# Attention score products over 80 and 81 rows or over all 128, with one column of the queries cleared

## The chip, the cores and the metric

The kernel runs on one core of a Trainium2 chip. The metric is the device time of one execution in microseconds (us). The core has TensorE (PE in the profile; its weight loads are PEld), VectorE (DVE), ScalarE (ACT), GpSimd (POOL) and SyncE (SP), which here only issues DMAs.

## What is computed

Clustered attention for 2 batches of 8 heads (768 tokens, 64 values a head), and behind it two feed-forward layers (512 to 2048 to 512) on the 1536 tokens:

```python
q_assign = np.argmax(np.einsum('bhsd,hcd->bhsc', q_n, c_n), axis=-1)   # 16 clusters, normalized rows
k_assign = np.argmax(np.einsum('bhsd,hcd->bhsc', k_n, c_n), axis=-1)
mask = q_assign[:, :, :, None] == k_assign[:, :, None, :]
scores = scale * np.matmul(q, k.transpose(0, 1, 3, 2))
scores = np.where(mask, scores, -1000000000.0)
scores = scores - np.max(scores, axis=-1, keepdims=True)
attn = np.exp(scores)
attn = attn / (np.sum(attn, axis=-1, keepdims=True) + 1e-09)
x = np.matmul(attn, v)          # heads side by side: 1536 x 512
x = softplus(x @ w_in) @ w_out
x = leaky_relu(x @ w_in2) @ w_out2
```

## The kernel before

The 16 heads are worked off one after the other, with the preparation of a head two heads ahead of its use. Each operation gets a priority (`at_pri`), and a scheduler, which models the times of all engines as the program is built, writes the order of each engine's instructions from the priorities and its own clock. Every engine then runs its list in that order. The feed-forward steps of the first batch are strewn between the heads of the second batch (`moe_steps`), so that TensorE has something to do; from about 300 us of the span on, the feed-forward layers stand alone.

For each head, queries and keys live in two padded fp16 buffers, `nq` and `nk`, of 128 partitions x 6 x 128 columns. Columns 0 to 63 hold the values (L293). Columns 64 to 79 hold the token's cluster as a one-hot row (L328, L329), scaled so that a pair of different clusters falls far down. Column 80 (`KS1`) of `nk` is always -1 (L742). Column 80 of `nq` takes the row maximum of the head, negated by that -1 in the product (L356), and columns 96 and 97 of `nq` take a flag for rows without a partner (L357). All other columns are zero from the start (L739). There are five `nq` buffers for the first batch and three for the second, and each is used again and again: `nq_87` by heads 0, 5, 8, 11 and 14, `nq_88` by 1, 6, 9, 12 and 15, `nq_89` by 2, 7, 10 and 13.

A head goes through these steps:

- `split` (L293 to L297): ACT writes the values into `nq` and `nk`; a DMA transpose gives `t1`.
- `assign_mm`, `assign_el` (L306 to L333): the cluster products on PE, the argmax in five DVE instructions that end with the one-hot `oh` (L325), ACT's two writes into `nq` and `nk`, and DMA transposes of both: `tq` (L332) and `tk` (L333).
- `emit_s1` (L344 to L351): the first score product, 12 matmuls of 384 columns, over the first `KS1` = 80 rows of `tq` and `tk`. DVE takes the maximum of each (L351). The two score banks `s1` in PSUM come free by that maximum alone.
- `emit_m` (L356 to L359): the maximum into column 80 of `nq`, the flag into columns 96 and 97, and one more DMA transpose of `nq`, now `tm`.
- `emit_s2` (L377, L378): the second score product, a full 128-row matmul for the low parts and one over `KS2` = 81 rows of `tk` and `tm`; ACT takes the exponential (L384) and POOL the low part of it (L386).
- `emit_pv` (L400 to L418) and `emit_norm`: times the values, and division by the sum.

Weights of the feed-forward layers are decoded from 64-bit to 32-bit numbers by DVE (L140 to L146) and split by ACT (L162) and DVE (L163) in between.

Of the kernel before, what the change touches and what calls it, by code (L numbers as in the profile page):

```python
# [30 lines left out]
NQ_BUFS, NK_BUFS, V_BUFS = (3, 2), (2, 1), 3  # L31
# [20 lines left out]
def by_group(table, h):  # L52
    return table[min(h // 2, 4 + (h >= 12))]
# [3 lines left out]
def attn_moe_kernel(  # L57
# [13 lines left out]
    V, S, G, PE = nc.vector, nc.scalar, nc.gpsimd, nc.tensor  # L71
    B, H, SEQ, D = q.shape
# [25 lines left out]
    def atile(shape, dt, tag, h):  # L98
        late, early = BUFS[tag]
        n = turn[tag] = turn.get(tag, -1) + 1  # L100
        if h < H and early and n % (late + early) >= late:
            return ep.tile(shape, dt, tag=tag, name=tag, bufs=early)
        return at.tile(shape, dt, tag=tag, name=tag, bufs=late)
# [23 lines left out]
    def ring(tag, h=NH):  # L127
        if h < H and tag == "s2":
            n = turn["ps" + tag] = turn.get("ps" + tag, -1) + 1
            if n % (PSUM_BUFS[tag] + 1) == PSUM_BUFS[tag]:  # L130
                return pm.tile([128, 512], F32, tag="m1", name="m")
        return pr.tile([128, 512], F32, tag=tag, name=tag, bufs=PSUM_BUFS[tag])
# [181 lines left out]
    def assign_el(h):  # L314
        nq, nk = nq_of[h], nk_of[h]
        aps = as_t.pop(h)
        a, e = (aps[:, n:n + 2 * C * NCL].rearrange("p (i j) -> p i j", j=NCL) for n in (0, 2 * C * NCL))
        mx = atile([128, 2 * C, 1], F32, "mx", h)
        V.reduce_max(out=mx, in_=a, axis=AX)
        V.tensor_tensor(out=e, in0=a, in1=mx.to_broadcast([128, 2 * C, NCL]), op=ALU.is_equal)  # L320
        V.tensor_tensor(out=e, in0=e, in1=tab, op=ALU.mult)
        m2 = atile([128, 2 * C, 1], F32, "m2", h)
        V.reduce_max(out=m2, in_=e, axis=AX)
        oh = atile([128, C, 2, NCL], F16, "oh", h)
        V.tensor_tensor(  # L325
            out=oh.rearrange("p c t j -> p (c t) j"), in0=e, in1=m2.to_broadcast([128, 2 * C, NCL]), op=ALU.is_equal
        )
        S.activation(out=nq[:, :, D:D + NCL], in_=oh[:, :, 0, :], func=AF.Copy, scale=BIG, bias=-BIG)  # L328
        S.activation(out=nk[:, :, D:D + NCL], in_=oh[:, :, 1, :], func=AF.Copy, scale=BIG)  # L329
        tk = atile([128, C, 128], F16, "tk", h)  # L330
        t = atile([128, C, 128], F16, "tq", h)
        nc.sync.dma_start_transpose(out=t, in_=nq.rearrange("p c d -> p (c d)"))  # L332
        nc.sync.dma_start_transpose(out=tk, in_=nk.rearrange("p c d -> p (c d)"))  # L333
        tp2[h] = t, tk

    KS1 = D + NCL
    KS2 = D + NCL + 1

    def emit_s1(h, c):
        t, tk = tp2[h]  # L340
        for j in range(2):
            bank = ring("s2" if h == 0 and j else "s1", h)
            o = bank[:, 0:3 * 128].rearrange("p (c r) -> p c r", c=3)
            PE.matmul(  # L344
                out=o,
                lhsT=t[0:KS1, c, :],
                rhs=tk[0:KS1, 3 * j:3 * j + 3, :],
                start=True,
                stop=True,
            )  # L350
            V.reduce_max(out=mms[h % 2][:, c, j:j + 1], in_=bank[:, 0:3 * 128], axis=AX)  # L351
# [10 lines left out]
    def emit_s2(h, kt):  # L362
        t1 = tp1[h].rearrange("p (c t) r -> p c t r", t=2)
        t2 = tp2[h][1]
        tqh = tpq[h]
        eng = by_group(PLO, h)[kt]
        p = atile([128, 2, 384], F32, "p", h)
        pl = atile([128, 2, 384], F16, "pl", h) if eng != "P" else None
        pb = p.bitcast(BF16).rearrange("p a (r t) -> p (a r t)", t=2)
        if eng == "D":  # L370
            pb = pb[:, 0:768].rearrange("p (a r) -> p a r", a=2)
        else:
            pb = pb.rearrange("p (a r t) -> p a r t", a=2, t=2)[:, :, :, 1]
        for j in range(2):
            sp = ring("s2", h)[:, 0:384]
            o = sp.rearrange("p (c r) -> p c r", c=3)
            PE.matmul(out=o, lhsT=t1[:, kt, 1, :], rhs=t1[:, 3 * j:3 * j + 3, 0, :], start=True, stop=False)  # L377
            PE.matmul(out=o, lhsT=t2[0:KS2, kt, :], rhs=tqh[0:KS2, 3 * j:3 * j + 3, :], start=False, stop=True)  # L378
            if eng == "D":
                S.activation(out=sp, in_=sp, func=AF.Exp, scale=scale)  # L380
                S.copy(out=pb[:, j, :], in_=sp)
                V.tensor_tensor(out=pl[:, j, :], in0=sp, in1=pb[:, j, :], op=ALU.subtract)
            else:
                S.activation(out=p[:, j, :], in_=sp, func=AF.Exp, scale=scale)  # L384
        if eng == "G":
            G.tensor_tensor(out=pl, in0=p, in1=pb, op=ALU.subtract)  # L386
        p_t[h, kt] = p, pb, pl
# [330 lines left out]
    with at_pri(-9):  # L718
# [6 lines left out]
            out=ss[:, 1:2], in0=ss[:, 0:1], scalar1=ss[:, 2:3], scalar2=ss[:, 1:2], op0=ALU.mult, op1=ALU.add  # L725
# [139 lines left out]
    def chain(h):  # L865
        if h < NH:
            with at_pri(h - LEAD_SPLIT):
                split(h)
            with at_pri(h - LEAD_ASSIGN):
                assign_mm(h)  # L870
                assign_el(h)
            with at_pri(h - LEAD_MAX):
                for c in range(C):
                    emit_s1(h, c)
            with at_pri(h - LEAD_M):
                emit_m(h)
            if h + 2 < NH:
                with at_pri(h - LEAD_LOAD):
                    load(h + 2)
# [12 lines left out]
    for h in range(NH):  # L892
        chain(h + AHEAD)
        wtie["h"] = h + 1
        with at_pri(h):
            if h + 1 < NH:
                split_v(h + 1)
            if h + 2 < NH:
                with behind_tm(h + 1):
                    load_v(h + 2)  # L900
            emit_sv(h)
        for j in range(C):
            with at_pri(h + j / 6):
                emit_s2(h, j)
                if j:
                    emit_pv(h, j - 1)
            if h < H - 1 and (j + h * C) % W_PER == 0:
                w_step()
            if h > H or (h == H and j > 0):
                moe_steps(FF_RATE)  # L910
            if h == H and j == 0:
                open_late()
        with at_pri(h + 1):
            emit_pv(h, C - 1)
            emit_empty(h)
        with at_pri(h + 1 - LEAD_NORM):
            emit_norm(h)
# [49 lines left out]
```

## Time and profile before

| | us |
|---|---|
| runs of the kernel (3) | 751.99, 756.89, 762.72 |
| median | 756.89 |
| the profiled execution's own time | 753.12 |
| its span, first to last instruction | 751.3 |
| mean granted TensorE clock over the span | 0.968 of full |

The span is what the rows below are read from; 1.8 us of the profiled execution's time lie around it. Rows are times in us from the start of the span. A granted clock of 1.00 is TensorE's upper level of 2.4 GHz, 0.50 the lower of 1.2 GHz. A matmul's duration runs from its start until its result is in PSUM, so matmuls that follow each other overlap, and busy time of PE says that something was in flight, not that it ran at its best.

### The profile page before, as it was taken

The page shows a single profiled execution, that of the slowest core. Times are in us where ns is not written, and L with a number is a line of the kernel's source. Part 1 is how long each engine was busy: PE and PEld are TensorE (multiplying, and loading weights), DVE is VectorE, ACT ScalarE, POOL GpSimd, SP SyncE. Part 2 cuts the span into 40 slices and gives each one's busy share as a digit, 9 for nine tenths or more (in the row PEclk, how much of TensorE's full clock was granted, in tenths as well). Part 3 has the DMA queues.
Part 4 walks back from the last instruction along what each step waited for, and adds up shares of the span by engine and source line. Part 5 has one row for each costly group of instructions (what it writes and reads, how often), then busy time and mean ns, then how long its engine had stood idle before and what let it go on. Part 6 is the DMA issues. An engine that isn't in the chain of part 4 may idle for free.

```text
span 751.3 us, 18834 instructions
## 1 busy us (share of the span) xinstructions
PE 689.3 (92%) x7488; PEld 509.8 (68%) x7488; DVE 515.0 (69%) x1154; ACT 402.6 (54%) x1071; POOL 400.0 (53%) x491
## 2 busy tenths in 40 slices
PE   1799888988888898999999999999999999999997
PEld 1368566655555565666666566656999999999996
DVE  4777667677788887029878866976476666666555
ACT  5465555566777766136335434534555555565553
POOL 4386567658788777211324342333646555656563
PEclk9988899998999999999999999999999999999999
DMA  8966656955785866012322355696100000000000
GB/s 199 195 133 148 127 124 108 189 123 126 185 186 141 156 155 161 14 22 66 120 96 64 106 181 169 181 357 218 74 2 30 2 30 2 30 2 30 2 30 29
DMA packets 118088, 81.01 MB, mean 108 GB/s; under 512 B 91888, under 2 KB 106224, under 8 KB 118000
## 3 DMA queue, kind: packets, MB, share of 16 engines
q1 hardware_dynamic: 117856, 79.55, 41.5%
q8 instruction: 58, 0.95, 0.5%
q14 instruction: 30, 0.25, 0.1%
q10 hardware_dynamic: 144, 0.26, 0.1%
HBM read 50.36 MB, written 10.49 MB: 81 GB/s over the span
## 4 chain that ended last, share of the span: by engine, by line
PE 55%; DVE 16%; DMA 12%; ACT 6%; POOL 5%; issue 4%; SPq 2%; DVEq 0%; POOLq 0%; ACTq 0%
PE i L538 13%; PE acc L538 13%; PE m L686 11%; PE m L673 6%; DMA t<-n 3%; DMA tm<-nq 2%; DMA v<-in_v_dram 2%; PE s L344 2%; PE s L378 2%; DMA st<-in_moe_w_in_dram 2%; DVE e L513 2%; PE s L377 2%; DVE w_in2l L240 2%; ACT p L384 2%; DVE g_l L487 1%
## 5 line engine op out<-in xcount | busy, mean ns | idle before, releaser
L386 POOL TENSOR_TENSOR pl<-p 128x768 f16<-128x768 f32 x88 | 128.3, 1467 | 56.2 <-ACT p L384 40.8
L351 DVE TENSOR_REDUCE mm<-s 128x1 f32<-128x384 f32 x190 | 101.2, 552 | 41.3 <-PE s L344 39.0
L538 PEld LDWEIGHTS <-w_in2h 128*128 128x128 f16 x1344 | 98.2, 98 | 5.3 <-issue 0.7
L546 DVE TENSOR_TENSOR gl<-r,gh 128x384 f16<-128x384 f32 (+1 forms) x96 | 63.8, 665 | 49.7 <-ACT gh L584 49.1
L384 ACT ACTIVATE p<-s 128x384 f32<-128x384 f32 x160 | 73.4, 493 | 29.1 <-PE s L378 25.4
L673 PE MATMUL m<-xth,w_inh 128*128 128x384 f16 x256 | 85.2, 333 | 3.4 <-ACT rl L497 1.8
L686 PE MATMUL m<-g_h,w_outh 128*128 128x384 f16 x256 | 84.3, 329 | 3.1 <-ACT w_outh L162 2.7
L686 PE MATMUL m<-g_l,w_outh 128*128 128x384 f16 x256 | 84.1, 328 | 2.1 <-DVE g_l L487 2.1
L673 PE MATMUL m<-xtl,w_inh 128*128 128x384 f16 x256 | 85.1, 333 | 0.0
L686 PE MATMUL m<-g_h,w_outl 128*128 128x384 f16 x256 | 84.0, 329 | 0.0
L546 POOL TENSOR_TENSOR r<-r,r 128x128 f32<-128x128 f32 x95 | 48.3, 526 | 55.7 <-ACT r L576 55.4
L673 PEld LDWEIGHTS <-w_inh 128*128 128x128 f16 x512 | 50.5, 100 | 36.9 <-issue 6.1
L344 PE MATMUL s<-tk,tq 80*128 80x384 f16 x190 | 65.0, 364 | 11.3 <-DMA tk<-nk 5.6
L686 PEld LDWEIGHTS <-w_outh 128*128 128x128 f16 x512 | 49.9, 99 | 37.2 <-ACT w_outh L162 3.6
L584 ACT CAST gh<-r 128x384 f16<-128x384 f32 (+1 forms) x96 | 54.2, 565 | 36.0 <-POOL r L546 32.6
L538 PEld LDWEIGHTS <-gh 128*128 128x128 f16 x672 | 60.5, 98 | 6.4 <-issue 1.1
L378 PE MATMUL s<-tm,tk 81*128 81x384 f16 x160 | 55.0, 354 | 8.7 <-DMA tm<-nq 8.7
L377 PE MATMUL s<-t 128*128 128x384 f16 x160 | 56.5, 353 | 3.7 <-ACT p L384 3.5
L200 POOL TENSOR_TENSOR wd<-wd 128x256 f32<-128x256 f32 x32 | 29.3, 924 | 54.5 <-DVE sg L194 39.8
L538 PE MATMUL i<-sh,w_in2h 128*128 128x128 f16 x384 | 53.5, 219 | 0.4 <-ACT r L576 0.4
L538 PE MATMUL i<-sl,w_in2h 128*128 128x128 f16 x384 | 53.5, 219 | 0.0
L538 PE MATMUL i<-sh,w_in2l 128*128 128x128 f16 x384 | 53.4, 219 | 0.0
(146 smaller groups left out, 1926.2 us busy)
## 6 DMA issues: line engine op xcount, KB each, us to landing
st<-in_moe_w_in_dram SPq DMA_DIRECT2D x32, 512.0 KB, 4.5
st<-in_moe_w_out_dram SPq DMA_DIRECT2D x32, 512.0 KB, 3.8
kept<-sg SPq DMA_DIRECT2D x16, 256.0 KB, 2.8
qk<-in_q_dram SPq DMA_DIRECT2D x16, 192.0 KB, 3.0
qk<-in_k_dram SPq DMA_DIRECT2D x16, 192.0 KB, 3.0
v<-in_v_dram SPq DMA_DIRECT2D x16, 192.0 KB, 4.2
kept<-sg SPq DMA_DIRECT2D x24, 128.0 KB, 2.8
out_dram<-ob SPq DMA_DIRECT2D x11, 256.0 KB, 2.3
```

What stands on the lines that cost most here:

```text
L200: G.tensor_tensor(out=out, in0=in0, in1=in1, op=ALU.subtract)
L344: PE.matmul(out=o, lhsT=t[0:KS1, c, :], rhs=tk[0:KS1, 3 * j:3 * j + 3, :], start=True, stop=True,)
L351: V.reduce_max(out=mms[h % 2][:, c, j:j + 1], in_=bank[:, 0:3 * 128], axis=AX)
L377: PE.matmul(out=o, lhsT=t1[:, kt, 1, :], rhs=t1[:, 3 * j:3 * j + 3, 0, :], start=True, stop=False)
L378: PE.matmul(out=o, lhsT=t2[0:KS2, kt, :], rhs=tqh[0:KS2, 3 * j:3 * j + 3, :], start=False, stop=True)
L384: S.activation(out=p[:, j, :], in_=sp, func=AF.Exp, scale=scale)
L386: G.tensor_tensor(out=pl, in0=p, in1=pb, op=ALU.subtract)
L538: one = PE.matmul(out=bank, lhsT=w_, rhs=x_, start=(first and i == 0), stop=(i == len(ops) - 1), skip_group_check=True)
L546: eng.tensor_tensor(out=out, in0=in0, in1=in1, op=op)
L584: S.copy(out=gh[:, lo:hi], in_=r[:, lo:hi])
L673: PE.matmul(out=hp, lhsT=w_, rhs=x_, start=(i == 0), stop=(i == len(ops) - 1))
L686: PE.matmul(out=yp, lhsT=w_[:, kk, ms], rhs=g_[:, kk, :], start=(n == 0), stop=(n == 3 * KFF - 1))
```

## The change

Both score products use all 128 rows of their operands. The rows that come in are zero in `tk` (columns 81 to 127 of `nk`), so they add nothing; but the first product now takes in row 80 as well, where `tk` holds -1, and `tq` would hold the maximum of the head that had the buffer before. So column 80 of `nq` is cleared by DVE ahead of the transpose, for the heads whose buffer was used before: heads 5, 6, 7 and 8 to 15, 11 in all.

```diff
@@ assign_el
+        if h >= (sum(NQ_BUFS) if h < H else H):
+            V.memset(nq[:, :, KS1:KS2], 0.0)
         S.activation(out=nq[:, :, D:D + NCL], in_=oh[:, :, 0, :], func=AF.Copy, scale=BIG, bias=-BIG)
@@ emit_s1
             PE.matmul(
                 out=o,
-                lhsT=t[0:KS1, c, :],
-                rhs=tk[0:KS1, 3 * j:3 * j + 3, :],
+                lhsT=t[:, c, :],
+                rhs=tk[:, 3 * j:3 * j + 3, :],
                 start=True,
@@ emit_s2
-            PE.matmul(out=o, lhsT=t2[0:KS2, kt, :], rhs=tqh[0:KS2, 3 * j:3 * j + 3, :], start=False, stop=True)
+            PE.matmul(out=o, lhsT=t2[:, kt, :], rhs=tqh[:, 3 * j:3 * j + 3, :], start=False, stop=True)
```

Lines from L328 on stand two lines further down in the changed kernel (the memset is its L329). The new instruction moves the scheduler's clock, so the lists of all engines differ in places from the middle of head 0 on.

On DVE, around the maximum of head 5 (`nq_87`), the kernel before has this order; `mm` are the maxima of the first score product, `svr` belongs to the sum of the values, `x` to the division of the head before:

```order
L351 TENSOR_REDUCE mm_101<-s_1587 128x1
L356 TENSOR_REDUCE nq_87<-mm_102 128x6
L351 TENSOR_REDUCE mm_101<-s_1590 128x1
L351 TENSOR_REDUCE mm_101<-s_1593 128x1
L430 SCALAR_TENSOR_TENSOR svr<-h_1941,sel,as 32x65
L351 TENSOR_REDUCE mm_101<-s_1596 128x1
L351 TENSOR_REDUCE mm_101<-s_1599 128x1
L351 TENSOR_REDUCE mm_101<-s_1602 128x1
L351 TENSOR_REDUCE mm_101<-s_1605 128x1
L447 TENSOR_SCALAR x<-x 128x6
```

At the same place the changed kernel has this:

```order
L358 TENSOR_REDUCE nq_87<-mm_102 128x6
L353 TENSOR_REDUCE mm_101<-s_1589 128x1
L353 TENSOR_REDUCE mm_101<-s_1592 128x1
L353 TENSOR_REDUCE mm_101<-s_1595 128x1
L353 TENSOR_REDUCE mm_101<-s_1598 128x1
L353 TENSOR_REDUCE mm_101<-s_1601 128x1
L432 SCALAR_TENSOR_TENSOR svr<-h_1944,sel,as 32x65
L329 MEMSET nq_87 128x6
L353 TENSOR_REDUCE mm_101<-s_1604 128x1
```

The memset for head 8 stands six instructions behind the maximum of head 5 in the same buffer. It may not overwrite the buffer before the transpose `tm` of head 5 has read it, and everything behind it on DVE waits as well.

On DVE, around the maximum of head 1 (`nq_88`), the kernel before has:

```order
L356 TENSOR_REDUCE nq_88<-mm_102 128x6
L351 TENSOR_REDUCE mm_101<-s_408 128x1
L351 TENSOR_REDUCE mm_101<-s_411 128x1
L319 TENSOR_REDUCE mx<-as 128x12
L351 TENSOR_REDUCE mm_101<-s_414 128x1
```

and the changed kernel:

```order
L358 TENSOR_REDUCE nq_88<-mm_102 128x6
L353 TENSOR_REDUCE mm_101<-s_405 128x1
L353 TENSOR_REDUCE mm_101<-s_408 128x1
L329 MEMSET nq_88 128x6
L353 TENSOR_REDUCE mm_101<-s_411 128x1
L319 TENSOR_REDUCE mx<-as 128x12
```

Here the memset for head 6 stands only two maxima behind the maximum of head 1. The other nine stand two to ten instructions behind the maximum of the head that had the buffer.

## Rows read from the trace of the kernel before

**Rows 1.** The page's slices of the span: granted clock in tenths
```profile
PEclk9988899998999999999999999999999999999999
```

**Rows 2.** Windows: stretch, its length, busy time of each engine, PEclk, DMA share, GB/s
```profile
30.00:300.00 270.00, 235.18 (x2940) 161.93 (x2940) 205.01 (x442) 173.15 (x428) 195.65 (x167) 0.92 0.67 149
300.00:751.00 451.00, 442.60 (x4427) 341.88 (x4423) 291.18 (x642) 215.58 (x609) 192.70 (x297) 1.00 0.24 78
```

**Rows 3.** The page's costliest groups: the three kinds of score matmul
```profile
L344 PE MATMUL s<-tk,tq 80*128 80x384 f16 x190 | 65.0, 364 | 11.3 <-DMA tk<-nk 5.6
...
L378 PE MATMUL s<-tm,tk 81*128 81x384 f16 x160 | 55.0, 354 | 8.7 <-DMA tm<-nq 8.7
L377 PE MATMUL s<-t 128*128 128x384 f16 x160 | 56.5, 353 | 3.7 <-ACT p L384 3.5
```

**Rows 4.** Windows of all engines, columns as in rows 2: three stretches and their successors
```profile
105.40:108.80 3.40, 2.26 (x23) 1.49 (x23) 1.30 (x4) 2.25 (x6) 1.64 (x2) 1.00 1.08 233
108.80:112.20 3.40, 3.40 (x22) 1.92 (x21) 1.51 (x4) 2.31 (x6) 2.39 (x3) 0.50 0.64 185
187.30:190.70 3.40, 2.31 (x33) 1.41 (x29) 0.08 (x1) 3.09 (x8) 3.40 (x4) 1.00 0.88 271
190.70:194.10 3.40, 1.29 (x16) 0.71 (x13) 2.27 (x4) 1.16 (x3) 1.91 (x2) 1.00 1.24 234
218.00:221.40 3.40, 1.79 (x26) 1.23 (x25) 3.21 (x7) 1.40 (x5) 1.80 (x3) 1.00 0.99 262
221.40:224.80 3.40, 3.40 (x41) 2.24 (x40) 2.52 (x6) 3.35 (x11) 3.33 (x4) 1.00 0.45 102
```

**Rows 5.** Windows of L344 on PE alone: busy time, PEclk, DMA share, GB/s
```profile
105.40:108.80 3.40, 0.87 (x4) 1.00 1.08 233
...
218.00:221.40 3.40, 0.65 (x2) 1.00 0.99 262
```

**Rows 6.** Windows of L378 on PE alone, columns as in rows 5
```profile
105.40:108.80 3.40, 1.30 (x5) 1.00 1.08 233
187.30:190.70 3.40, 1.31 (x4) 1.00 0.88 271
218.00:221.40 3.40, 0.74 (x3) 1.00 0.99 262
```

**Rows 7.** The chain, shares of 50.7-61.0, 78.1-84.9, 108.8-112.2, 173.6-180.5, in this order
```profile
by line: PE x L400 25.4%; PE s L344 17.0%; PE s L377 9.3%; PE x L413 9.1%; PE x L414 8.9%; PE x L418 6.4%; PE s L378 6.2%; DVE wcp L143 5.9%; DVE mm L351 4.6%; PE m L377 3.1%; PE m L378 3.1%; PE as L425 3.1%; PE as L424 2.7%; issue 0.4%
by line: PE s L377 25.9%; PE s L378 23.5%; PE s L344 18.4%; PE m L378 11.8%; PE m L377 11.1%; PE x L436 6.5%; PE x L418 4.9%; issue 0.3%
by line: PE s L344 23.9%; PE s L377 18.8%; PE s L378 18.8%; PE m L377 16.8%; PE x L413 9.8%; PE x L414 9.6%; PE m L378 9.4%
by line: DMA t<-n 102.3%; PE m L673 49.9%; PE as L306 11.7%; PE s L377 9.5%; PE s L378 9.3%; PE s L344 9.3%; issue 0.7%
```

**Rows 8.** Line L742: the only small memset of one column
```profile
L742 DVE MEMSET nk<- x3: 63/63/63, 8.3 to 8.4; 128x6 f16 x3
```

**Rows 9.** Timeline of DVE, 100.5 to 108: start, duration, instruction, idle time before it
```profile
100.71 0.18 DVE L356 TENSOR_REDUCE nq<-mm 128x6 f16<-128x18 f32 x1
...
103.50 1.53 DVE L351 TENSOR_REDUCE mm<-s 128x1 f32<-128x384 f32 x3 [0.32 <-PE s L344]
107.39 0.56 DVE L351 TENSOR_REDUCE mm<-s 128x1 f32<-128x384 f32 x1 [2.36 <-PE s L344]
```

**Rows 10.** The chain, 100 to 108: start, duration, what
```profile
102.24 4.26 DMA tm<-nq
```

**Rows 11.** Timeline of DVE, 41.5 to 46
```profile
43.67 0.36 DVE L319 TENSOR_REDUCE mx<-as 128x12 f32<-128x192 f32 x1 [0.22 <-PE as L306]
```

**Rows 12.** Timeline of ACT, 44 to 46
```profile
44.74 0.51 ACT L293 CAST nq<-qk 128x384 f16<-128x384 f32 x1 [0.63 <-DMA tm<-nq]
```

**Rows 13.** Waits of the whole span: us in total, times, longest
```profile
ACT nq L293 <- DMA tm<-nq: 14.1, 9, 3.0
```

## Prediction

> **What bounds the kernel now.** I read the page's clock line first [rows 1], then two windows that split the span [rows 2], then the chain of waits within single stretches. The clock line has its eights in the first third only and nines behind it. The windows say the same in numbers: from 300 us on PE is busy for 442.6 of 451 us at a clock of 1.00, and nothing in this change touches that part. From 30 to 300 us, where the heads run, PE is busy for 235.2 of 270 us at a mean clock of 0.92, and DVE for 205.0, ACT for 173.2, POOL for 195.7. No engine is full there: the chain goes from transposes (one is 4.26 us long [rows 10]) to PE, to DVE's maxima, to ACT's exponentials, and back. So a gain has to come from 30 to 300 us, and the mean clock bounds it: 0.92 at levels of 1.00 and 0.50 means that 0.08 / 0.50 x 270 = 43 us are run at half clock. If PE set the end through all of these, full clock would give back half, 21.6 us. That is the most the clock can give.
>
> **The change part by part.**
>
> *The matmuls themselves.* There are 192 matmuls in L344 and 192 in L378. Their duration doesn't speak for a price of the rows: 364 ns with 80 rows, 354 with 81, and 353 for L377 with all 128 and the same 384 columns [rows 3]. So I put the additional rows at 0 ns. Both sides: 353 - 364 = -11 ns times 384 is -4 us of busy time, 353 - 354 = -1 ns times 384 is -0.4 us; the differences are those of the clock in which the groups happened to run, so no term.
>
> *What the rows may do to the clock.* The granted clock falls behind stretches in which PE has little to do. Three stretches can be compared [rows 4]. From 105.4 to 108.8 PE was busy for 2.26 us, and the clock was 0.50 in the next stretch. From 187.3 to 190.7 it was busy for 2.31 us, and the clock stayed. From 218.0 to 221.4 it was busy for only 1.79 us, and the clock stayed too. So busy time doesn't sort them. What differs is the kind of work: in the first, 4 + 5 = 9 of 23 matmuls were score matmuls over 80 or 81 rows, with 0.87 + 1.30 us of busy time [rows 5, 6]; in the second 4 of 33 (L378's alone), in the third 2 + 3 = 5 of 26. The clock fell where most of the work was done by part of the rows. If what counts is work in rows, the change makes each of these matmuls count for 128, and stretches like the first keep their clock. The Trainium skill speaks against it (TensorE: Matmul & The Clock Gate, section "What's actually happening"): the clock follows how busy PE has been of late, with no word of rows. By that rule alone the change does nothing to the clock, and the term that follows is 0; the three stretches here don't agree with busy time alone, but they are only three.
>
> The price comes from the chain. Four half-clock stretches lie behind waits in which score matmuls of part of the rows were a good part of PE's work: 50.7 to 61.0, 78.1 to 84.9, 108.8 to 112.2 and 173.6 to 180.5. PE's shares of the chain there add up to 94%, 102%, 107% and 90% [rows 7] (pieces at the edges count whole, so a sum can pass 100). Half of that time would go at full clock: 0.94 x 10.3 / 2 = 4.9, 1.02 x 6.8 / 2 = 3.5, 1.07 x 3.4 / 2 = 1.8 and 0.90 x 6.9 / 2 = 3.1, in sum 13.3 us. The rest of the 21.6 us lies in stretches that follow waits with few score matmuls, which should stay, or in which PE isn't on the chain. Of the 13.3 us I take half, 6.6: once PE is quick again, what is late next is DVE's maxima, which are 552 ns apiece against 160 ns for the 384 columns of a matmul at 2.4 GHz, and the two score banks come free by them alone. Ends: 0 and -21.6 us.
>
> *The memset.* Eleven instructions of one column; the like of it took 63 ns [rows 8], so 0.7 us on DVE. Its wait is dearer. Each stands few instructions behind the maximum of the head that had the buffer, and may start only once that head's transpose `tm` has landed. Behind it stand the maxima of the head that is then prepared, behind those PE's next L344 (two banks), and behind that PE's other work, since PE takes its list in order. For head 8: the maximum of head 5 was at 100.71, the rows up to the memset were through at 103.50 + 1.53 = 105.03 [rows 9], and the transpose landed at 102.24 + 4.26 = 106.50 [rows 10]. The memset would wait 1.5 us, but DVE did nothing until 107.39 anyway: PE was itself behind that transpose. There the wait is covered. For head 6 it isn't: DVE went on to L319 at 43.67 [rows 11], and the transpose landed at about 44.74, when ACT's write into the same buffer was released [rows 12]: 1.1 us of DVE lost. ACT's write has the same wait at all places, and there it costs 14.1 us at 9 of them [rows 13]. So the memsets' waits cost DVE between 0 (all covered as at head 8) and some 14 us (none covered). Head 6 is the kind I expect at about a third of the places, 11 / 3 x 1.1 = 4 us of DVE, of which less than half should reach the end, because DVE has 270 - 205 = 65 us of idle time in these stages [rows 2]: 1.5 us, its own 0.7 us included.
>
> *The moved order.* The lists of all engines differ locally; I see no side in it, cost it at 0 and allow 5 us either way.
>
> *The sum.* -6.6 + 1.5 = -5.1 us against the profiled execution's own 753.1 us: 748.0. The median of the runs lies 3.8 us above that execution, so 756.9 - 5.1 = 751.8, in round numbers 752 us.
>
> **The rivals.**
>
> *The rows don't count for the clock.* For it: only three stretches speak for rows, and the third, with the least busy time, kept its clock with 5 score matmuls. Against it: the first has more busy time than the third and fell. Then only the memset is left: 756.9 + 1.5 = 758.4, with the moved order 754 to 764. This is also the case in which the rule of the skill's page holds.
>
> *The memsets' waits decide: slower.* The place is the memset in DVE's list, the price the 14.1 us that ACT loses at the same landings. It decides if DVE comes to the memset before the landing at most of the 11 places and PE isn't itself behind that transpose, so that maxima that would have been made in the wait are late, the two banks stay full, and PE starves at just the place where its clock falls. With no clock gained: 756.9 + 14.1 + 0.7 = 771.7, and each additional half-clock stretch like that at 108.8 adds 1.8 us: up to about 775. For it: head 6, and ACT's longest wait of 3.0 us. Against it: head 8, and DVE's idle time.
>
> *All half clock goes.* If the clock holds through the heads and PE sets the end in these stretches, -21.6 + 1.5 = -20.1 us: 736.8; with a part of it hidden by DVE, about 740. Against it: waits for transposes and weights remain, and stretches without score matmuls such as 190.7 to 194.1 (busy for 1.29 us) gain nothing by rows.
>
> **How the numbers follow.** The forecast has a chance of 0.52 and a range of its own of 745 to 758; the rows that don't count 0.24; the waits 0.11; all half clock gone 0.13. The range of 738 to 769 takes in the first two cases whole and reaches into the other two. A difference of 2% is 15.1 us, about what a measurement of this kernel can tell from no change: faster than 741.8 is most of the last case and a little of the forecast, 0.14; slower than 772.0 is the upper half of the waits' case and what a bad order could add, 0.09; within 2% is what remains, 0.77.
>
> **What would show it.** Right: the clock over 30 to 300 us rises from 0.92 to 0.95 or more, the half clock at the like of 50.7 to 61.0 and 108.8 to 112.2 is gone, L346 and L380 (the new lines of the score matmuls) keep their duration at full clock, and the memsets of L329 last 0.06 us with a few us of DVE idle ahead of them by DMA `tm`. The feed-forward part from 300 us on keeps its length. Wrong: a clock that stays at 0.92 (rows don't count), DVE idle at the memsets in sum near 14 us with PE waiting for `mm` behind it (the waits decide), a clock near 1.00 (all of it goes), or a clock that rises while the heads end no sooner, which would say that PE's speed in those stretches was covered by DVE and the transposes, and that half was too much to take.

## The result, and the profile after

The changed kernel takes 758.46 us (median of 22 runs, 753.57 to 761.75) against 754.44 us for the kernel before on the same chips (749.18 to 762.72). The ratio is 1.0054, with a 95% interval of 1.0033 to 1.0074: 4 us slower, where 5 us faster was forecast. The time lies inside the range, well within 2%, but on the other side of 1. Here and below, times are medians of all executions, and ratios leave out those more than 1.5% above the fastest of their kernel (the profiles of runs 2 and 11 are of such executions, and aren't read).

The profiled execution has a span of 755.9 us. Its clock line, in 40 slices as in [rows 1]:

```profile
PEclk9899999899999999999999999999999999999999
```

Of the four eights in the first third, two are left. In windows, columns as in [rows 2], the heads and the feed-forward part:

```profile
30.00:300.00 270.00, 226.19 (x2931) 156.10 (x2931) 198.96 (x445) 172.38 (x426) 195.82 (x167) 0.95 0.69 145
300.00:756.00 456.00, 443.89 (x4433) 342.58 (x4430) 296.95 (x650) 216.35 (x611) 192.78 (x297) 0.99 0.24 79
```

The clock over the heads rose from 0.92 to 0.95, as the prediction asked. PE's busy time there fell from 235.2 to 226.2 us. But PE also got fewer matmuls done by 300 us, 2931 against 2940, and what is left to do behind 300 us takes 456 us and not 451. PE's time was gained on each matmul and lost between them.

The groups of the page that answer to [rows 3]:

```profile
L346 PE MATMUL s<-tk,tq 128*128 128x384 f16 x190 | 61.6, 345 | 14.0 <-DMA tk<-nk 7.5
...
L380 PE MATMUL s<-tm,tk 128*128 128x384 f16 x160 | 53.0, 339 | 10.8 <-DMA tm<-nq 10.8
L379 PE MATMUL s<-t 128*128 128x384 f16 x160 | 53.6, 337 | 7.5 <-ACT p L386 6.7
```

All three kinds are shorter, L379 too, which the change doesn't touch: that is the clock. The rows themselves have no price. But the idle time of PE ahead of each has grown: from 11.3, 8.7 and 3.7 us (L344, L378, L377) to 14.0, 10.8 and 7.5 (L346, L380, L379).

The memsets, by their line and what DVE waited for ahead of them:

```profile
L329 DVE MEMSET nq<- x11: 63/63/63, 33.0 to 236.9; 128x6 f16 x11
its engine sat idle before it (us, times) until:
  DMA tm<-nq: 4.8, 4
```

63 ns each, and 4.8 us of waits at 4 of 11 places: the size that the prediction drew from head 6 (4 us at a third of the places).

### The profile page after: what moved, and what is told of

Same layout as the page of the kernel before. It is cut to its first block, busy times and chain, and to the rows that moved or that the text cites. A ratio compares the mean times of both kernels' runs of the same rounds, so it can differ in the third digit from the quotient of the medians.

```text
span 755.9 us, 18867 instructions
## 1 busy us (share of the span) xinstructions
PE 680.3 (90%) x7488; PEld 504.2 (67%) x7488; DVE 514.8 (68%) x1165; ACT 402.7 (53%) x1071; POOL 400.3 (53%) x491
## 4 chain that ended last, share of the span: by engine, by line
PE 51%; DMA 17%; DVE 15%; ACT 6%; issue 4%; POOL 4%; SPq 2%; DVEq 0%; POOLq 0%; ACTq 0%
PE acc L540 13%; PE i L540 13%; PE m L675 9%; PE m L688 7%; DMA v<-in_v_dram 3%; DMA t<-n 3%; DMA tm<-nq 3%; DMA st<-in_moe_w_in_dram 3%; DMA st<-in_moe_w_out_dram 2%; DVE mm L353 2%; DMA tk<-nk 2%; PE s L346 2%; DVE w_in2l L240 1%; DVE e L515 1%; PE s L380 1%
## 5 line engine op out<-in xcount | busy, mean ns | idle before, releaser
L346 PE MATMUL s<-tk,tq 128*128 128x384 f16 x190 | 61.6, 345 | 14.0 <-DMA tk<-nk 7.5
L380 PE MATMUL s<-tm,tk 128*128 128x384 f16 x160 | 53.0, 339 | 10.8 <-DMA tm<-nq 10.8
L379 PE MATMUL s<-t 128*128 128x384 f16 x160 | 53.6, 337 | 7.5 <-ACT p L386 6.7
L415 PE MATMUL x<-v,p 128*128 128x65 f16 x528 | 49.8, 198 | 5.4 <-DVE y L452 4.9
```

Source lines behind the costliest of these rows:

```text
L346: PE.matmul(out=o, lhsT=t[:, c, :], rhs=tk[:, 3 * j:3 * j + 3, :], start=True, stop=True,)
L380: PE.matmul(out=o, lhsT=t2[:, kt, :], rhs=tqh[:, 3 * j:3 * j + 3, :], start=False, stop=True)
L415: PE.matmul(out=o, lhsT=pb[:, cs], rhs=v2[:, kt, D:2 * D + 1], start=(kt == 0 and c == 0), stop=False)
```

## The experiments

The experiments separate three things that the change does at once: the rows on the chip, the memset, and the order of the lists. For that some kernels change the rows of the finished matmuls after the scheduler has written its lists, with this helper at the end of the program (`have` picks the matmuls and weight loads, `want` gives their rows):

```python
def rows(have, want):
    for bb in nc.main_func.blocks:
        done = []
        for i in bb.instructions:
            if i.opcode in ("Ldweights", "Matmult") and have(i):
                ins = [type(x)(ap=[(x.ap[0][0], want(i))] + list(x.ap[1:]), offset=x.offset, ...) for x in i.ins]
                i = i.__replace__(ins=ins)
            done.append(i)
        bb.instructions = done
```

Ratios are to the kernel before, run on the same chip in turn.

### 1. The order of before, all 128 rows

```diff
+    rows(lambda i: i.ins[0].ap[0][1] in (80, 81), lambda i: 128)
     r = _run(nc, [arrays], core_ids=[0])
```

> Order of before on every engine, instruction for instruction; only the rows of the two score matmuls are 128 in place of 80 and 81. There is no memset, so in the first product row 80 takes in the maximum of the head that had the buffer before (that part of the computation differs). Theory A (the rows keep the clock up and this is worth time; the loss of the changed kernel is from its moved order): 3 to 7 us faster than before, ratio 0.991 to 0.996, mean clock 0.98 or more. Theory B (the memsets' waits on DVE cost): the same as A here. Theory C (the clock goes up, but what PE gains is covered by transposes and DVE): ratio 0.998 to 1.002 with a clock of 0.98. Theory D (rows don't count for the clock; the rise to 0.978 came from the moved order): clock stays at 0.965 to 0.970, ratio 1.000.

Measured: 749.33 us, ratio 0.9923 (0.9894 to 0.9953). The rows alone, in the same order, are worth 0.77%, 5.8 us. Theory A or B; C (the gain is covered) and D (rows don't count) fall. The clock of before and of this run over the same stretch, first before, then this run (from 37.1 us on, since before's trace holds no clock events earlier):

```profile
37.10:300.00 262.90, 230.24 (x2906) 159.07 (x2905) 201.53 (x433) 169.00 (x417) 192.36 (x164) 0.92 0.67 147
```
```profile
37.10:300.00 262.90, 224.77 (x2935) 155.71 (x2934) 200.93 (x434) 169.76 (x418) 194.22 (x165) 0.96 0.67 149
```

0.08 / 0.50 x 262.9 = 42 us at half clock become 0.04 / 0.50 x 262.9 = 21 us. PE is 5.5 us less busy and has done 29 matmuls more. These are single executions; over the executions of both kernels the median of the mean granted clock rises from 0.970 to 0.981, which is some 16 us of half clock rather than 21.

Single stretches of this run, to be held against those of the prediction:

```profile
50.00:58.00 8.00, 7.49 (x132) 6.07 (x132) 7.87 (x19) 5.50 (x15) 8.00 (x7) 1.00 0.99 190
104.80:108.20 3.40, 3.40 (x16) 1.71 (x15) 2.32 (x7) 2.40 (x6) 1.56 (x3) 0.50 0.95 241
170.00:176.50 6.50, 5.47 (x62) 3.36 (x59) 6.29 (x16) 6.02 (x15) 5.84 (x6) 1.00 0.56 164
```

What ran at half clock from 50.7 to 61.0 and from 173.6 to 180.5 now runs at full clock. The stretch behind the wait that the prediction used as its main example (105.4 to 108.8, now about 3 us earlier) still ran at half: the reason was right in sum, and its own showpiece doesn't bear it out. The two places aren't quite alike, though: half clock now sets in a little earlier in the work, and PE was busy for only 1.40 of the 3.4 us ahead of it, where it had been 2.26.

### 2. The order of the changed kernel, 80 and 81 rows

```diff
+    rows(lambda i: i.debug.lineno in (346, 380), lambda i: {346: 80, 380: 81}[i.debug.lineno])
     r = _run(nc, [arrays], core_ids=[0])
```

> Order and memset of the changed kernel, instruction for instruction; the score matmuls take 80 and 81 rows as before. A: slower than before by 1.0 to 1.5% (the moved order without the rows' gain), clock 0.96. B: likewise 1.0 to 1.5%. C: about 1.005, as with all rows, at a clock of 0.96. D: 1.005 and a clock of 0.978 as in the changed kernel.

Measured: 765.84 us, ratio 1.0097 (1.0054 to 1.0141). Without the rows' gain the changed kernel would be a full percent slower. The granted clock, as the median over the executions that the ratios take, closes the square: 0.970 in both orders with 80 and 81 rows, 0.981 (order of before) and 0.982 (changed order) with 128. So between these two orders the clock follows the rows and not the order (run 6 has a third order, where it rose less), and the loss is in what remains: the memset or the order.

### 3. The memset tied behind its own one-hot

```diff
-        V.tensor_tensor(
+        last = V.tensor_tensor(
             out=oh.rearrange("p c t j -> p (c t) j"), ...
         if h >= (sum(NQ_BUFS) if h < H else H):
-            V.memset(nq[:, :, KS1:KS2], 0.0)
+            with tc.issue_after(last.ins):
+                V.memset(nq[:, :, KS1:KS2], 0.0)
```

> The changed kernel with the memset tied behind the one-hot of its own head, so that it comes one to two heads later in DVE's list, long after the transpose it must wait for. B: DVE's waits for the transpose at the memset (4.8 us at 4 places in the changed kernel) go to 0, and the time falls to a ratio of 0.996 to 1.001. A: the waits go too, but the order moves again, and the time may land anywhere between 0.995 and 1.010; it says nothing alone. C: 1.003 to 1.007, as the changed kernel.

Measured: 758.58 us, ratio 1.0052 (1.0024 to 1.0080), the changed kernel's own. The waits are gone, as the line of the memset shows:

```profile
L330 DVE MEMSET nq<- x11: 63/63/63, 69.7 to 267.8; 128x6 f16 x11
its engine sat idle before it (us, times) until:
who waited for it (us, times):
  ACT nq L331: 0.9, 1
```

No DVE time ahead of it, and no time won. That speaks against B, though the order has moved a little as well; the next run has no such gap.

### 4. The memset at the same place, without the wait

```diff
+    for bb in nc.main_func.blocks:
+        ...
+            if i.opcode == "Memset" and i.debug.lineno == 329:
+                i = i.__replace__(outs=[o], sync_info=type(s)(on_wait=[], on_update=s.on_update))
```

`o` is six elements a partition in the tile `sq`, which nobody reads any more.

> The changed kernel's order, instruction for instruction, with all 128 rows; the 11 memsets stand at the same places of DVE's list but write into a tile nobody reads any more and wait for nothing. So the column isn't cleared, and the first product takes in the old maximum (that part of the computation differs). B: the loss goes, ratio 0.996 to 1.001, since 4.8 us of DVE waits are gone. A: stays at 1.003 to 1.006, since the order is what costs. C: 1.003 to 1.006 too; e1 tells C from A.

Measured: 759.75 us, ratio 1.0058 (1.0029 to 1.0087). Every list is the changed kernel's, 4.8 us of DVE waits are gone, and the time is the same. B falls: within the interval the memsets' waits cost nothing, so they are covered, as at head 8 in the prediction.

### 5. Column 80 cleared by ACT, order of before

```diff
-        oh = atile([128, C, 2, NCL], F16, "oh", h)
+        oh = ohs[h % 2]      # two fixed tiles of NCL + 1 columns, the last set to 1.0 at the start
-            out=oh.rearrange("p c t j -> p (c t) j"), ...
+            out=oh.rearrange("p c t j -> p (c t) j")[:, :, 0:NCL], ...
-        S.activation(out=nq[:, :, D:D + NCL], in_=oh[:, :, 0, :], func=AF.Copy, scale=BIG, bias=-BIG)
+        S.activation(out=nq[:, :, D:D + NCL + 1], in_=oh[:, :, 0, :], func=AF.Copy, scale=BIG, bias=-BIG)
+    rows(lambda i: i.ins[0].ap[0][1] in (80, 81), lambda i: 128)
```

> All 128 rows without the memset and, but for 6 rows of difference near the end of PE's list and the places of a few instructions at the start, in the order of before: the one-hot gets a 17th column that is always 1, ACT's write of the cluster takes it along (32768 x 1 - 32768 = 0) and so clears column 80; the scheduler still sees 80 and 81 rows, and the rows are set to 128 behind it. Theory A (rows gain about 6 us, the moved order costs about 7): ratio 0.989 to 0.996, clock 0.98, faster than both kernels. Rival (the gain of the first run came from the old maximum in row 80 or from the missing clear): 0.998 or more.

Measured: 752.07 us, ratio 0.9953 (0.9922 to 0.9984): faster than before and than the changed kernel, with nothing of the computation left out. It stands a little above the first run (0.9923), but the intervals overlap; this version's clock was 0.976 in the median, between the two levels of the other runs.

### 6. The order that the memset alone makes

The changed source with 80 and 81 rows for the scheduler, and 128 set behind it:

```diff
-                lhsT=t[:, c, :],
+                lhsT=t[0:KS1, c, :],
...
+    rows(lambda i: i.ins[0].ap[0][1] in (80, 81), lambda i: 128)
```

> All 128 rows and the memset, but in the order that the scheduler makes when it sees 80 and 81 rows and the memset; this differs from before's and from the changed kernel's. A1 (what costs in the changed kernel's order is what the row counts did to it): like the first run with the order of before, 0.990 to 0.998. A2 (any move of the order costs, the tuned one being the best of many): 1.000 to 1.006.

Measured: 755.98 us, ratio 1.0001 (0.9972 to 1.0031). Neither clean case: 0.8% above the order of before with the same rows, and 0.5% below the changed kernel. A third order gives back what the rows gain, but not more. Its clock was 0.972 in the median, against 0.970 for the kernel before and 0.976 to 0.979 for the other kernels with 128 rows on the same chip (runs 5, 7 and 8): in this order the rows raised the clock by little. So orders differ by about as much as the rows are worth, and the order also has a say in how much clock the rows give.

### 7. All 128 rows, scheduled as such, no memset

```diff
-        if h >= (sum(NQ_BUFS) if h < H else H):
-            V.memset(nq[:, :, KS1:KS2], 0.0)
```

> All 128 rows, scheduled as such, without the memset: every engine's list is that of the changed kernel, less the 11 memsets on DVE (the first product takes in the old maximum, that part of the computation differs). A: the loss is all in the order that the row counts make, ratio 1.002 to 1.007, as the changed kernel. B (the memset costs, by its wait or otherwise): 1.000 or below.

Measured: 760.85 us, ratio 1.0073 (1.0041 to 1.0105). The lists of PE, ACT, POOL and SP are those of the changed kernel to the instruction, DVE's too but for the 11 memsets. So it isn't the memset that made the changed kernel's order. The row counts alone made the scheduler write other lists, though a matmul over them lasts as long on the chip; what in its model of the engines reacts to the rows stays open.

### 8. Only the second product over 128 rows

```diff
-            PE.matmul(out=o, lhsT=t2[0:KS2, kt, :], rhs=tqh[0:KS2, 3 * j:3 * j + 3, :], start=False, stop=True)
+            PE.matmul(out=o, lhsT=t2[:, kt, :], rhs=tqh[:, 3 * j:3 * j + 3, :], start=False, stop=True)
```

> Only the second product over all 128 rows, the first over 80 as before; no memset is needed. The scheduler's lists differ from before's from head 8 on, hardly ahead of it. A with the loss put between heads 4 and 7 (where the changed kernel loses 8 of its 10 us against the same rows in the order of before): about half of the rows' gain and little loss, 0.993 to 0.999. If the order's loss isn't tied to that place: 1.000 or more.

Measured: 752.82 us, ratio 0.9968 (0.9938 to 0.9997). One line of source, no memset, no helper, and faster than before by 0.3%. All rows that are added here hold zeros in `tk`; the clock was 0.979, against 0.970 for the kernel before on the same chip.

### 9 and 10. Which half of the heads has the loss

`emit_s1` and `emit_s2` take 128 rows where the condition holds and `KS1` or `KS2` where it doesn't; all are set to 128 behind the scheduler.

```diff
+        k1 = 128 if h < H else KS1        # run 10: h >= H
-                lhsT=t[0:KS1, c, :],
+                lhsT=t[0:k1, c, :],
```

> All 128 rows on the chip in all heads, no memset (the first product takes in the old maximum, that part of the computation differs). The scheduler sees 128 rows for heads 0 to 7 and 80 or 81 for heads 8 to 15: the lists are the changed kernel's up to the preparation of head 8, and go their own way behind it. If the order's loss is made ahead of head 8 (theory A with the place at heads 4 to 7): 1.002 to 1.008. If it is made behind: 0.990 to 0.997.

> The reverse: the scheduler sees 80 or 81 rows for heads 0 to 7 and 128 for heads 8 to 15; all are run with 128, no memset (the same part of the computation differs). The lists are before's up to the preparation of head 8. Loss ahead of head 8: 0.989 to 0.996, like the order of before with 128 rows (0.992). Loss behind it: 1.002 or more.

Measured: 1.0033 (1.0002 to 1.0064; 760.96 us) with the changed kernel's lists up to the preparation of head 8, and 0.9952 (0.9917 to 0.9988; 753.12 us) with before's lists up to there. Most of the order's loss is made in the first batch: 1.0033 / 0.9923 = 1.1% in run 9 and 0.9952 / 0.9923 = 0.3% in run 10, the latter inside the intervals. The split is a rough one, since behind head 8 run 9 has lists of its own and not the changed kernel's.

The five lists of run 10 are also those of run 8, instruction for instruction; the two differ in the rows of the first product alone. Their ratios, 0.9952 and 0.9968, and clocks, 0.978 and 0.979, can't be told apart: in this order the second product's rows give what both give.

The place can be seen in the normalization of a head (its product with 1 / sum on DVE). Head 3 and head 7 in the first run, in the order of before with 128 rows:

```profile
92.49 0.56 DVE L450 TENSOR_TENSOR y<-x,dd 128x384 f32<-128x384 f32 x1
...
151.75 0.55 DVE L450 TENSOR_TENSOR y<-x,dd 128x384 f32<-128x384 f32 x1
```

and in the changed kernel:

```profile
94.35 0.56 DVE L452 TENSOR_TENSOR y<-x,dd 128x384 f32<-128x384 f32 x1
...
161.72 0.55 DVE L452 TENSOR_TENSOR y<-x,dd 128x384 f32<-128x384 f32 x1
```

1.9 us behind at head 3, 10.0 us behind at head 7, the last of the first batch. Runs 9 and 10 fall on the two sides: head 7 at 160.8 and at 150.3. The first matmul of the feed-forward work, which fills PE's gaps from then on, comes 10.1 us later too, at 151.6 against 141.5, and the spans of the two kernels differ by 755.9 - 746.3 = 9.6 us in the end. That the loss stays because nothing filled PE's gaps ahead of it is an argument; no run tests it.

The windows between these two points show what PE did, first in the order of before, then in the changed kernel:

```profile
92.50:151.80 59.30, 49.73 (x699) 36.07 (x696) 42.28 (x101) 33.10 (x85) 40.65 (x34) 0.94 0.69 137
```
```profile
94.30:161.70 67.40, 53.33 (x715) 38.86 (x714) 44.66 (x106) 37.26 (x93) 44.05 (x38) 0.92 0.69 129
```

Of the 8.1 us, PE was idle for 4.5 (14.07 against 9.57) and busy for 3.6, at a clock that was lower there, 0.92 against 0.94. The chain between these two points, first in the order of before (92.5 to 151.8), then in the changed kernel (94.3 to 161.7):

```profile
by line: DMA tm<-nq 18.1%; DMA t<-n 15.4%; ACT p L384 8.0%; issue 7.1%; PE s L378 5.8%; PE s L344 5.3%; PE x L400 4.5%; PE s L377 4.5%; POOL pl L386 4.2%; PE as L306 3.7%; PE x L418 2.7%; PE m L377 2.6%; PE x L413 2.3%; PE x L414 2.2%; PE m
```
```profile
by line: DMA v<-in_v_dram 22.5%; DMA tm<-nq 16.9%; DMA tk<-nk 6.8%; ACT p L386 6.3%; PE s L346 6.1%; PE x L402 5.7%; PE s L380 5.6%; issue 5.2%; PE s L379 4.5%; DVE mm L353 3.4%; PE x L415 2.5%; PE x L416 2.2%; PE x L420 1.8%; SPq L361 1.8%
```

The loads of `v` head the second list and are nowhere near the top of the first. On ACT, whose list holds the cast of `v` (L285) at fixed places, that looks so in the changed kernel:

```profile
112.17 0.52 ACT L285 CAST v<-v 128x384 f16<-128x384 f32 x1 [3.08 <-DMA v<-in_v_dram]
...
133.37 0.52 ACT L285 CAST v<-v 128x384 f16<-128x384 f32 x1 [1.57 <-DMA v<-in_v_dram]
```

and in the order of before at the like of the first of them:

```profile
109.90 0.51 ACT L285 CAST v<-v 128x384 f16<-128x384 f32 x1
```

There the cast comes when `v` has long landed; in the changed kernel ACT stands before it for 3.08 and 1.57 us, with exponentials behind it in its list. All waits of this kind between the two points, in the first run and in the changed kernel:

```profile
ACT v L285 <- DMA v<-in_v_dram: 2.0, 2, 1.1
```
```profile
ACT v L285 <- DMA v<-in_v_dram: 6.8, 3, 3.1
```

### 11 and 12. Shorter loads of v in both orders

```diff
+            if i.opcode.startswith("DMA") and i.debug.lineno == 280:      # from the fourth head on
+                a = [(6 * a[0][0], 128)] + a[1:] if a[0][1] == 768 else [a[0], (a[1][0], 1), a[2]]
```

> The changed kernel, every list as it is, with the loads of v from the fourth head on cut to a sixth of their bytes (the other tokens' values are then those of an earlier head; that part of the computation differs). In the changed order ACT waits 6.8 us for v within heads 4 to 7, in the order of before with 128 rows 2.0 us. Theory V (these waits are what the order costs there): 4 us or more faster than the changed kernel, ratio 0.996 to 1.000, and the distance to the next run falls from 9 us to 5 or less. Rival (v only happens to stand on the chain, and another transpose takes its place): both kernels gain alike, ratio 1.000 to 1.004 here, distance 7 to 10 us.

> The control: the order of before with all 128 rows (the first run), with the same cut of the loads of v. V: little changes, 0.989 to 0.993. Rival: it gains as much as the run beside it, 0.985 to 0.991.

Measured: 1.0022 (0.9989 to 1.0055; 757.24 us) in the changed order, 0.9919 (0.9889 to 0.9949; 749.64 us) in the order of before. Against the same orders with whole loads (1.0054 and 0.9923) the first gained 0.3%, the control nothing. The distance fell from 1.3% to 1.0%, 7.8 us: inside the rival's band and far above the 5 us that theory V set. The control, which gained nothing, falls in V's band and not in the rival's, so neither theory has it whole. `v` on the chain is at most a part of it, some 2 us by the ratios and not clear of their intervals. What the rest of the first batch's loss comes from stays open; that the order makes it is shown by runs 1, 7, 9 and 10.

## Why the prediction was wrong

**The step that failed is the moved order**, in the prediction's words: "The lists of all engines differ locally; I see no side in it, cost it at 0 and allow 5 us either way." With 128 rows in both, the changed lists cost 1.0054 / 0.9923 = 1.3%, 9.9 us, against 0 and about twice the allowance; with 80 and 81 rows in both they cost 1.0%, 7.3 us (run 2). Nor was it the memset that moved them, as the section on the change has it: the row counts alone give the same lists (run 7).

The other terms, against what the runs gave:

| term | forecast | measured |
|---|---|---|
| rows on PE | 0 | 0: 339 and 345 ns against 337 for an untouched group |
| rows, by the clock | -6.6 us (0 to -21.6) | -5.8 us in the order of before (0.9923); -0.43%, 3.2 us, in the changed order (1.0054 / 1.0097), where the intervals overlap |
| memset and its waits | +1.5 us (0 to +14) | 0 within the intervals (1.0058 and 1.0073 against 1.0054) |
| moved order | 0 (5 either way) | +9.9 us with 128 rows, +7.3 us with 80 and 81 |

-5.8 + 9.9 = +4.1 us, the 0.54% measured; it comes out by construction, since the 9.9 us are the difference of the other two, and 7.3 - 3.2 = 4.1 us is the same sum the other way round. The clock's term was right in its mechanism, in its sign and nearly in its size. The guess that half of what PE gains is covered can't be pinned down: in the two profiles 42 - 21 = 21 us of half clock went, which would be 10.5 us if PE set the end throughout, while the medians over the executions (0.970 and 0.9805) give 0.0105 / 0.50 x 750 = 16 us and so 8 us; 5.8 us came. The rival that rows don't count is refuted, and with it, for this kernel, the reading of the Trainium skill's sentence (TensorE: Matmul & The Clock Gate, "What's actually happening") by which only PE's busy time would matter: with every list the same, 80 and 81 rows gave 0.970 and 128 rows 0.981. The evidence was weaker than the conclusion, though: of the three stretches that were compared, the one that carried the argument didn't change in run 1. And in the changed kernel half clock isn't quite gone from the like of 50.7 to 61.0, where the prediction wanted none: the clock reads 0.57 from 50 to 54 us and 1.00 from 54 to 62.

The memset's cost was looked for in the right place, and its waits came as worked out (4.8 us of DVE), but within the interval they cost nothing, which fits the 65 us that DVE has to spare there. The rival built on them fell by run 4.

The section on what would show the forecast wrong named "a clock that rises while the heads end no sooner". That came for the first batch only: its last normalization is at 161.7 us, against 154.7 before. The last head of all ends sooner, at 318.5 against 332.4 (both behind 300 us, where the heads' part was taken to end), with less of the feed-forward work done by then. These are head 7 and head 15 before, and head 15 in the changed kernel:

```profile
154.66 0.55 DVE L450 TENSOR_TENSOR y<-x,dd 128x384 f32<-128x384 f32 x1
...
332.41 0.56 DVE L450 TENSOR_TENSOR y<-x,dd 128x384 f32<-128x384 f32 x1
```
```profile
318.45 0.55 DVE L452 TENSOR_TENSOR y<-x,dd 128x384 f32<-128x384 f32 x1
```

And the reason it gave, that PE's speed was covered, is not the reason. In the order of before PE's speed was worth nearly what was forecast. The first batch ended later because the engines' lists of the changed kernel take longer from head 4 to head 7; what in them does it is known only in part.

The prediction had this order before it. It showed the DVE lists of two places and read from them only the new instruction, not how far the other engines' lists had moved ahead of head 8, where nothing fills PE's gaps. A term that rearranges all five lists can't be given a narrower range than the terms that it is added to. With 10 us either way the sum would have been -5 with ends of -15 and +5, and the honest forecast one of no difference.

## What to carry to other kernels

An edit that changes an instruction's shape may change the order of the whole program where a scheduler writes it from modelled times, even if the instruction lasts as long as before on the chip: run the edit once in the old order, so that its own effect and the order's can be told apart. Here the two were of opposite sign and of like size. And look at an order ahead of the filler work first: of the two orders compared here, the one that was 10.0 us behind there was 9.6 us behind at the end. That isn't the only place: run 6 reached head 7 at 149.2 us, ahead of run 1's 151.8, and still took 0.8% longer.

## What was not expected of the hardware

Zero rows count for the clock. The rows that were added hold zeros in `tk` (all but row 80 of the first product), and still the granted clock rose from 0.970 to 0.981 with every instruction at its place (run 1), and half of the half-clock time of the heads went in the profiles compared. Run 8, whose added rows are all zero, reads 0.979, in an order that differs from before's behind head 8. The price in PE time was nil.

A granted clock of 1.00 in a row isn't always a reading. Before's trace shows 1.00 from 30.0 to 37.1 us, ahead of its first clock event. Its matmuls there say otherwise:

```profile
33.55 0.53 PE L344 MATMUL s<-tk,tq 80*128 80x384 f16 x1
```

0.53 us for what takes 0.326 us at full clock; the first run shows 0.50 for the like stretch. The 0.92 of [rows 2] is therefore a little too high, and the windows above begin at 37.1.
